# A fused attention and feed-forward kernel: a hand-woven schedule re-ordered, with sums moved from VectorE to GpSimd

## The chip, the core and the metric

The kernel runs on one core of a Trainium2 chip. The metric is the device time of one execution in microseconds (us), the median of several runs. Five engines with queues of their own work on it: TensorE (PE, matrix products), VectorE (DVE), ScalarE (ACT), GpSimd (POOL) and SyncE (SP, which issues most DMA transfers). Each engine takes its instructions strictly in the order in which the program gives them; an instruction that waits for another engine holds up everything behind it in its own queue.

## The reference

Inputs are q, k, v of shape (4 batches, 8 heads, 768 positions, 64), a decay per head, and the weights `w_in` (512 x 2048), `w_out` (2048 x 512) and `alpha` (2048).

```
for each block b of 64 positions:                        # causal linear attention with decay
    out[b]   = ((q_b k_b^T) * Dmask) v_b + (q_b * lam_pow) kv_state
    kv_state = lam^64 * kv_state + (k_b * rev_pow)^T v_b
x = out, heads side by side                              # 3072 x 512
h = x @ w_in                                             # 3072 x 2048
g = max(h, 0) + alpha * min(h, 0)
return g @ w_out                                         # 3072 x 512
```

## The kernel before

The 3072 rows are cut into six chunks `c` of 512 rows (256 positions of two batches). Every chunk goes through three steps.

**Attention.** A chunk has four groups `n` (a batch and four heads), so chunk 5 has the groups 20 to 23. `prepared(n)` casts q and k, loads v and multiplies k by its decay (`key_decayed`, GpSimd, L291). `turned(n)` transposes by DMA, `decayed(n)` multiplies the transposed q by its decay (GpSimd, L355). `cluster(old, new)` is one attention group on TensorE: the state part and the scores times v of group `old`, the scores and the new state of group `new`. Behind it VectorE masks the scores (`masked`, L402) and updates the state (`states`, L465), and ScalarE copies the result into the chunk's input for the next step (`attended`, L250).

**Up** (`up(c, f)`, L545, L553, L560): 16 pieces for a chunk, each four products 128x512 into one of two PSUM banks "h". ScalarE makes relu(-h) from the bank, then VectorE makes g from both (here "the g step"). The bank comes free with the g step, so an up piece waits for the g step of the up piece two before it.

**Down.** For the chunks 3, 4 and 5 the product g @ w_out is done with seven products of quarter matrices in place of eight (`down2`, `down2_last`, L655). A11, A12, A21, A22 are quarters of g and B11 to B22 quarters of `w_out`. Four sums of g are needed: S1 = A21 + A22, S3 = A11 - A21, S2 = S1 - A11, S4 = A12 - S2 (`g_sum`, L638; all but S1 overwrite a quarter). Each comes in four parts (0 to 3), one for every two of the eight 128-column blocks of a quarter. Four sums of weights are needed once: three new tiles W0, W1, W2 and B22 - B12 in the place of B12, called W3 here (`weight_sum`, L621), again in four parts. All of these are elementwise instructions of 128x512 values of 16 bits. The seven products are used in the order 1, 2, 6, 5, 7, 3, 4, each in two halves of eight matmuls (d = 0 to 13). Product 6 reads S2, product 5 reads S1, product 7 reads S3 and W3, product 3 reads S4, product 4 reads W2. S1 has one buffer, so the S1 of the next chunk is written after product 5 of this one.

**The order.** The queue order is written out by hand. For the last three chunks a loop weaves three things: up pieces of chunk c, down pieces of chunk c-1, and (from a table `plan`) the attention of chunk c+1. `order[c]` is a string of U (up) and D (down) pieces; for c = 4 and c = 5 it has 30 pieces with two U's side by side once in the middle. `sums_at` says after which piece a part of S2 or S4 is put in the queue, and `sums13` puts parts of S1 and S3 in the queue after the 10th, 12th, 14th and 16th up piece. The loop of c = 4 is called the woven stage below and that of c = 5 the next stage; after them `down2_last` does the down step of chunk 5 alone.

In the kernel before, S1 and S3 are on GpSimd (letter "G") and S2, S4 and all weight sums on VectorE ("V").

Of the kernel before, what the change touches and what calls it, by code (L numbers as in the profile page):

```python
# [11 lines left out]
def kernel(  # L12
# [16 lines left out]
    nc = tc.nc  # L29
# [5 lines left out]
    ALU = mybir.AluOpType  # L35
# [124 lines left out]
    for half in range(2):  # L160
# [7 lines left out]
        out=drop, in0=rel_i, scalar1=0.0, scalar2=-1e30, op0=ALU.is_lt, op1=ALU.mult  # L168
# [115 lines left out]
    def engine(x):  # L284
        return nc.gpsimd if x == "G" else nc.vector
# [82 lines left out]
    def inter(n):  # L368
        co, bo, ho = units[n]
        pbo, bb = co // 2, 2 * (co % 2) + bo  # L370
        for a in range(2):
            if 2 * pbo + a == 0:
                continue
            for hp in range(2):
                nc.tensor.matmul(  # L375
                    ot[a][:, hp, :].rearrange("p (e j) -> p e j", e=2),
                    lhsT=R[bb, ho, 2 * pbo + a][:, hp].rearrange("p l d -> p (l d)"),
                    rhs=T[n]["qdT"][:, :, hp, ds(a * 64, 64)],
                    start=(hp == 0),
                    stop=False,  # L380
                    skip_group_check=True,
                )

    def score_products(n):
        t = T[n]
        t["s"] = ps.tile([128, 2, 2, 2, L], fp32, tag="s", name="s")
        for hp in range(2):
            for e in range(2):
                for a, hl in QUADS:
                    p = ds(hl * 64, 64)  # L390
                    nc.tensor.matmul(  # L391
                        t["s"][ds(a * 64, 64), hl, hp, 1 - e, :].rearrange("p (e j) -> p e j", e=2),
                        lhsT=t["qkT"][p, 1, e, hp, ds(a * 64, 64)],
                        rhs=t["qkT"][p, 0, :, hp, ds(a * 64, 64)],
                        start=True,
                        stop=True,
                    )

    def masked(n):
        t = T[n]  # L400
        t["sm"] = sm_pool.tile([128, 2, 2, 2, L], fp16, tag="sm", name="sm")
        nc.vector.tensor_tensor(  # L402
            out=t["sm"].rearrange("p a h x j -> p (a h) x j"),
            in0=t["s"].rearrange("p a h x j -> p (a h) x j"),
            in1=mask_of(units[n][2]),
            op=ALU.mult,
        )

    def intra(n):
        t = T[n]  # L410
        pb = units[n][0] // 2
        for hp in range(2):
            for e in range(2):
                for hl, a in QUADS:
                    p = ds(a * 64, 64)
                    nc.tensor.matmul(  # L416
                        ot[a][ds(hl * 64, 64), hp, :],
                        lhsT=t["v16"][p, 2 * hp + hl, e, :],
                        rhs=t["sm"][p, hl, hp, 1 - e, :],
                        start=(2 * pb + a == 0 and hp == 0 and e == 0),  # L420
                        stop=(e == 1),
                        skip_group_check=True,
                    )
# [5 lines left out]
    def state_products(n, kv, fresh, blocks=None):  # L429
        t = T[n]  # L430
        for hp in range(2):
            for e in range(2):
                for hl in range(2):
                    for a in blocks or blocks_of(n):
                        p = ds(a * 64, 64)
                        nc.tensor.matmul(  # L436
                            kv[a][ds(hl * 64, 64), hp, hl, :],
                            lhsT=t["kdec"][p, e, 2 * hp + hl, :],
                            rhs=t["v16"][p, 2 * hp + hl, e, :],
                            start=(fresh and hp == 0 and e == 0),  # L440
                            stop=(e == 1),
                            skip_group_check=True,
                        )

    def attended(n, eng):
        co, bo, ho = units[n]
        if co not in XT:
            XT[co] = xt_pool.tile([128, NHP, 2, 2, L], fp16, tag="xT", name="xT")
        copy_on(
            eng,  # L450
            XT[co][:, ds(2 * ho, 2), :, bo, :].rearrange("p h e (a j) -> p a (h e) j", a=2),
            acc[:, :, 0:256].rearrange("p a (he j) -> p a he j", j=64),
        )
# [24 lines left out]
    def cluster(old, new, eng="A"):  # L478

        if old is not None:  # L480
            inter(old)
        if new is not None:
            score_products(new)
        if old is not None:
            intra(old)
        if new is not None:
            state_products(new, kv_acc, old is None)
            masked(new)
        if old is not None:
            attended(old, eng)  # L490
        if new is not None:
            states(new, kv_acc)
# [35 lines left out]
    G = {}  # L528
# [83 lines left out]

    halves = [[w_out_sb[:, ds(8 * x, 8), ds(256 * y, 256)] for y in range(2)] for x in range(2)]

    def weight_sum(i, part):

        p = ds(2 * part, 2)
        (b11, b12), (b21, b22) = [[y[:, p] for y in x] for x in halves]
        w = [sums[x][:, p] for x in range(3)]
        out, in0, in1 = [(w[0], b12, b11), (w[1], b22, w[0]), (w[2], b21, w[1]), (b12, b22, b12)][i]  # L620
        nc.vector.tensor_tensor(out=out, in0=in0, in1=in1, op=ALU.subtract)  # L621

    def part_of(c, j, half, e, b=None):
        x = group_of(c, j)[:, half, :, e]
        return x.rearrange("p i b j -> p i (b j)") if b is None else x[:, :, b]

    def g_sum(c, i, j, eng, b=None):

        a11, a12, a21, a22 = [part_of(c, j, half, e, b) for e in range(2) for half in range(2)]
        s1 = sums[3].rearrange("p f (b j) -> p f b j", b=2)[:, ds(2 * j, 2)]  # L630
        s1 = s1.rearrange("p i b j -> p i (b j)") if b is None else s1[:, :, b]
        out, in0, in1, op = {
            1: (s1, a21, a22, ALU.add),
            3: (a21, a11, a21, ALU.subtract),
            2: (a11, s1, a11, ALU.subtract),
            4: (a12, a12, a11, ALU.subtract),
        }[i]
        engine(eng).tensor_tensor(out=out, in0=in0, in1=in1, op=op)  # L638
# [82 lines left out]
    def sums13(c, j, eng="G"):  # L721
        g_sum(c, 1, j, eng)
        g_sum(c, 3, j, eng)
# [303 lines left out]
    def prepared(n):  # L1027
        casts(n, "AA")

    def turned(n):  # L1030
        transposes(n, "D", False)

    plan = {
        3: {
            0: lambda: (turned(18), load(5, 0, "k"), load(5, 0, "q"), decayed(17)),
            2: lambda: prepared(19),
            4: lambda: cluster(16, 17),
            7: lambda: (turned(19), decayed(18)),
            10: lambda: prepared(20),
            11: lambda: cluster(17, 18),  # L1040
            13: lambda: (turned(20), decayed(19), load(5, 1, "k"), load(5, 1, "q")),
# [6 lines left out]
        },  # L1048
        4: {
            2: lambda: prepared(23),  # L1050
            4: lambda: cluster(20, 21),
            7: lambda: (turned(23), decayed(22)),
            11: lambda: cluster(21, 22),
            13: lambda: decayed(23),
            18: lambda: cluster(22, 23),
            25: lambda: cluster(23, None),
        },
        5: {},
    }
    order = {c: "U" + "DU" * 7 + "U" + "DU" * 7 for c in plan}  # L1060
    order[3] = "UD" * 16
    sums_at = {3: (2, 0), 4: (2, 1), 5: (2, 2), 6: (2, 3), 11: (4, 0), 12: (4, 1), 13: (4, 2), 14: (4, 3)}
    sum_tiles()
    for c, at in plan.items():
        u = d = 0
        for x, what in enumerate(order[c]):
            if x in at:
                at[x]()
            if what == "U":
                up(c, u // 2 + 8 * (u % 2), None, "h")  # L1070
                u += 1
                if u in (10, 12, 14, 16):
                    sums13(c, u // 2 - 5)
            elif c == 3:
                down(c - 1, d // 4, d % 4, 4, ("op", "tk")[d // 4 % 2])
                d += 1
                if d > 2 and d <= 14:
                    weight_sum(*divmod(d - 3, 4))
            else:
                down2(c - 1, d)  # L1080
                d += 1
            if c > 3 and x in sums_at:
                g_sum(c - 1, *sums_at[x], "V")
            if c == 4 and 7 <= x <= 10:
                weight_sum(3, x - 7)
    down2_last(NC - 1)


# [28 lines left out]
```

## Time and profile before

| | |
|---|---|
| median of 3 runs | 209.15 us (208.95 to 209.23) |
| profiled execution | 209.0 us, of which 207.1 us are the span from the first to the last instruction |
| TensorE busy | 200.2 us (97% of the span) |
| VectorE busy | 158.4 us (76%) |
| ScalarE busy | 113.6 us (55%) |
| GpSimd busy | 112.6 us (54%) |
| granted TensorE clock, mean | 0.997 |

The profile is one execution. Busy time of TensorE is modelled at the ends of matmuls, so how fast TensorE goes is better read from the start times of its pieces. In a timeline a row gives start, duration, engine, line and operation, and in brackets how long the engine was idle before it and who released it.

### The profile page before, as it was taken

The page shows a single profiled execution, that of the slowest core. Times are in us where ns is not written, and L with a number is a line of the kernel's source. Part 1 is how long each engine was busy: PE and PEld are TensorE (multiplying, and loading weights), DVE is VectorE, ACT ScalarE, POOL GpSimd, SP SyncE. Part 2 cuts the span into 40 slices and gives each one's busy share as a digit, 9 for nine tenths or more (in the row PEclk, how much of TensorE's full clock was granted, in tenths as well). Part 3 has the DMA queues.
Part 4 walks back from the last instruction along what each step waited for, and adds up shares of the span by engine and source line. Part 5 has one row for each costly group of instructions (what it writes and reads, how often), then busy time and mean ns, then how long its engine had stood idle before and what let it go on. Part 6 is the DMA issues. An engine that isn't in the chain of part 4 may idle for free.

```text
span 207.1 us, 5564 instructions
## 1 busy us (share of the span) xinstructions
PE 200.2 (97%) x2263; PEld 121.4 (59%) x2263; DVE 158.4 (76%) x285; ACT 113.6 (55%) x210; POOL 112.6 (54%) x134
## 2 busy tenths in 40 slices
PE   7999999999999999999999999998999999999993
PEld 6776445556445465555555455475667666666782
DVE  7978889477789657899989996769976467855740
ACT  7986778154777118656757456472553544534221
POOL 8999793054486883294447985292074140462400
PEclk9999999999999999999999999999999999999998
DMA  5999999997999996989899973151101111011122
GB/s 154 281 195 232 246 260 207 234 285 230 244 257 265 200 259 142 235 134 172 138 138 264 229 151 89 25 114 12 54 3 51 66 38 51 2 51 59 47 101 101
DMA packets 58061, 31.16 MB, mean 150 GB/s; under 512 B 27108, under 2 KB 55796, under 8 KB 58036
## 3 DMA queue, kind: packets, MB, share of 16 engines
q1 hardware_dynamic: 42884, 21.25, 42.4%
q0 software_dynamic: 15136, 9.57, 29.0%
q8 instruction: 17, 0.28, 0.6%
q14 instruction: 8, 0.07, 0.1%
q10 hardware_dynamic: 16, 0.00, 0.0%
HBM read 27.27 MB, written 6.29 MB: 162 GB/s over the span
## 4 chain that ended last, share of the span: by engine, by line
PE 83%; DVE 10%; ACT 2%; issue 2%; POOL 1%; POOLq 1%; ACTq 0%
PE h_ps L545 37%; PE o_ps L573 19%; PE o_ps L655 14%; PE s L391 3%; PE acc L416 3%; PE acc L375 2%; DVE g L638 2%; DVE g L560 2%; DVE sm L402 2%; PE tpx L341 2%; DVE dmask L202 1%; PE acc L436 1%; DVE R L465 1%; DVE w_out_sb L621 1%; ACT L180 1%
## 5 line engine op out<-in xcount | busy, mean ns | idle before, releaser
L545 PE MATMUL h_ps<-xT,w_in_sb 128*128 128x512 f16 (+1 forms) x392 | 92.1, 375 | 1.0 <-DVE g L560 0.8
L560 DVE SCALAR_TENSOR_TENSOR g<-m,oma,h_ps 128x512 f16<-128x512 f32 (+1 forms) x98 | 71.1, 733 | 26.5 <-ACT m L553 23.5
L553 ACT ACTIVATE m<-h_ps 128x512 f32<-128x512 f32 (+1 forms) x98 | 57.3, 588 | 49.0 <-PE h_ps L545 44.7
L545 PEld LDWEIGHTS <-w_in_sb 128*128 128x128 f16 x392 | 37.5, 98 | 38.5 <-issue 1.7
L573 PE MATMUL o_ps<-w_out_sb,g 128*128 128x512 f16 x192 | 46.8, 380 | 0.0
L402 DVE TENSOR_TENSOR sm<-s,dmask 128x1024 f16<-128x1024 f32 x24 | 29.2, 1218 | 11.4 <-PE s L391 11.4
L638 POOL TENSOR_TENSOR s<-g 128x512 f16<-128x512 f16 x12 | 14.4, 1198 | 40.5 <-DVE g L560 25.7
L655 PEld LDWEIGHTS <-g 128*128 128x128 f16 x288 | 27.7, 98 | 9.2 <-DVE g L638 0.8
L573 PEld LDWEIGHTS <-g 128*128 128x128 f16 x192 | 17.6, 98 | 19.4 <-DVE g L560 0.2
L250 ACT ACTIVATE xT<-acc 128x512 f16<-128x512 f32 x24 | 14.3, 598 | 23.4 <-PE acc L436 20.4
L355 POOL TENSOR_TENSOR qdT<-qkT,qdecay 128x512 f16<-128x512 f16 (+1 forms) x19 | 20.9, 1107 | 6.0 <-DMA qkT<-qk 6.0
L655 PE MATMUL o_ps<-w_out_sb,g 128*128 128x256 f16 x192 | 24.1, 273 | 0.0
L291 POOL TENSOR_TENSOR kdec<-kraw,kdecay 128x512 f16<-128x512 f32 x18 | 19.5, 1088 | 6.6 <-DMA kraw<-in_k_dram 6.5
L254 POOL CAST qk<-qraw 128x512 f16<-128x512 f32 x12 | 7.8, 652 | 17.6 <-DMA qraw<-in_q_dram 17.6
L465 DVE SCALAR_TENSOR_TENSOR R<-R,rdecay,acc 128x128 f16<-128x128 f16 x54 | 15.4, 339 | 0.1
L278 POOL DMA_DIRECT2D v<-in_v_dram x19 | 14.9, 791 | 0.4 <-issue 0.4
L638 POOL TENSOR_TENSOR g<-g 128x512 f16<-128x512 f16 x12 | 14.1, 1171 | 0.9
L685 ACT ACTIVATE o_sb<-o_ps 128x512 f32<-128x512 f32 (+1 forms) x16 | 7.9, 491 | 11.7 <-PE o_ps L655 11.7
L655 PE MATMUL o_ps<-w_sum,g 128*128 128x256 f16 x96 | 12.6, 273 | 0.3 <-DVE g L638 0.3
L391 PE MATMUL s<-qkT 64*64 64x128 f16 x384 | 10.1, 221 | 0.1
L416 PE MATMUL acc<-sm,v 64*64 64x128 f16 x384 | 9.8, 218 | 0.1
L254 POOL CAST qk<-kraw 128x512 f16<-128x512 f32 x9 | 5.5, 613 | 6.7 <-DMA kraw<-in_k_dram 3.9
(80 smaller groups left out, 191.6 us busy)
## 6 DMA issues: line engine op xcount, KB each, us to landing
out_dram<-o_sb SPq DMA_DIRECT2D x20, 256.0 KB, 2.8
kraw<-in_k_dram SPq DMA_DIRECT2D x7, 512.0 KB, 5.5
qraw<-in_q_dram SPq DMA_DIRECT2D x6, 512.0 KB, 5.7
v<-in_v_dram POOLq DMA_DIRECT2D x19, 128.0 KB, 6.0
w_in_sb<-in_moe_w_in_dram POOLq DMA_DIRECT2D x4, 512.0 KB, 8.5
w_out_sb<-in_moe_w_out_dram POOLq DMA_DIRECT2D x4, 512.0 KB, 10.6
qraw<-in_q_dram POOLq DMA_DIRECT2D x6, 256.0 KB, 7.2
qraw<-in_q_dram SPq DMA_DIRECT2D x6, 256.0 KB, 4.6
```

Source lines behind the costliest of these rows:

```text
L291: engine(eng).tensor_tensor(out=kdec, in0=kr, in1=kdecay[:, ds(4 * hh, 4), :].rearrange("p h e -> p e h").unsqueeze(3).to_broadcast([128, ...
L355: engine(eng).tensor_tensor(out=qdT[:, :, :, p], in0=(t["qps"] if eng == "P" else t["qkT"][:, 0])[:, :, :, p], in1=qdecay[:, hh, :, :, p], ...
L391: nc.tensor.matmul(t["s"][ds(a * 64, 64), hl, hp, 1 - e, :].rearrange("p (e j) -> p e j", e=2), lhsT=t["qkT"][p, 1, e, hp, ds(a * 64, 64)] ...
L402: nc.vector.tensor_tensor(out=t["sm"].rearrange("p a h x j -> p (a h) x j"), in0=t["s"].rearrange("p a h x j -> p (a h) x j"), in1=mask_of ...
L416: nc.tensor.matmul(ot[a][ds(hl * 64, 64), hp, :], lhsT=t["v16"][p, 2 * hp + hl, e, :], rhs=t["sm"][p, hl, hp, 1 - e, :], start=(2 * pb + a ...
L465: nc.vector.scalar_tensor_tensor(out=R[b, hh, m + 1][:, hp], in0=R[b, hh, m][:, hp], scalar=rdecay[:, 2 * hh + hp : 2 * hh + hp + 1], in1= ...
L545: nc.tensor.matmul(h_ps[:, 0:n] if bi is None else h_ps[:, 0:n].rearrange("p (e j) -> p e j", e=2), lhsT=w_in_sb[:, gi, ts(f, 128)], rhs=x ...
L553: nc.scalar.activation(m[:, 0:n], h_ps[:, 0:n], AF.Relu, scale=-1.0)
L560: nc.vector.scalar_tensor_tensor(out=g, in0=mv, scalar=oma[:, f : f + 1], in1=hv, op0=ALU.mult, op1=ALU.add)
L573: nc.tensor.matmul(o_ps, lhsT=lhs(c, f, t), rhs=w_out_sb[:, f, :], start=(f == 0), stop=(f == NF - 1),)
L638: engine(eng).tensor_tensor(out=out, in0=in0, in1=in1, op=op)
L655: nc.tensor.matmul(t[:, cols], lhsT=x, rhs=w, start=(fresh and f == 0), stop=(last and f == NF // 2 - 1), skip_group_check=True,)
```

## The change

For the woven stage (c = 4) and the next stage (c = 5):

- the two U's side by side move from the pieces 14 and 15 to 18 and 19 of the 30 (counted from 0);
- the attention groups in c = 4 go from in front of the pieces 4, 11, 18 and 25 to in front of 8, 14, 22 and 28;
- in c = 4, the parts 1 and 3 of S2 and all of S4 go to GpSimd, and S4 from the pieces 11 to 14 to the pieces 15, 17, 19 and 21;
- in c = 5, S2 stays and S4 goes to the pieces 11, 13, 15 and 17, still on VectorE;
- W2 goes from VectorE in the loop of c = 3 to GpSimd in c = 4 (after the pieces 10, 12, 14 and 16), W3 from the pieces 7 to 10 to 10 to 13, still on VectorE;
- the last part of S1 and S3 (chunk 5, after its last up piece) goes from GpSimd to VectorE.

```diff
-    def weight_sum(i, part):
+    def weight_sum(i, part, eng="V"):
...
-        nc.vector.tensor_tensor(out=out, in0=in0, in1=in1, op=ALU.subtract)
+        engine(eng).tensor_tensor(out=out, in0=in0, in1=in1, op=ALU.subtract)
...
         4: {
             2: lambda: prepared(23),
-            4: lambda: cluster(20, 21),
             7: lambda: (turned(23), decayed(22)),
-            11: lambda: cluster(21, 22),
+            8: lambda: cluster(20, 21),
             13: lambda: decayed(23),
-            18: lambda: cluster(22, 23),
-            25: lambda: cluster(23, None),
+            14: lambda: cluster(21, 22),
+            22: lambda: cluster(22, 23),
+            28: lambda: cluster(23, None),
         },
         5: {},
     }
-    order = {c: "U" + "DU" * 7 + "U" + "DU" * 7 for c in plan}
+    order = {c: "U" + "DU" * 9 + "U" + "DU" * 5 for c in plan}
     order[3] = "UD" * 16
-    sums_at = {3: (2, 0), 4: (2, 1), 5: (2, 2), 6: (2, 3), 11: (4, 0), 12: (4, 1), 13: (4, 2), 14: (4, 3)}
+    sums_at = {
+        4: {3: (2, 0, "V"), 4: (2, 1, "G"), 5: (2, 2, "V"), 6: (2, 3, "G")},
+        5: {3: (2, 0, "V"), 4: (2, 1, "V"), 5: (2, 2, "V"), 6: (2, 3, "V")},
+    }
+    for x in range(4):
+        sums_at[4][15 + 2 * x] = (4, x, "G")
+        sums_at[5][11 + 2 * x] = (4, x, "V")
...
                 if u in (10, 12, 14, 16):
-                    sums13(c, u // 2 - 5)
+                    sums13(c, u // 2 - 5, "V" if c == 5 and u == 16 else "G")
...
-                if d > 2 and d <= 14:
+                if d > 2 and d <= 10:
                     weight_sum(*divmod(d - 3, 4))
...
-            if c > 3 and x in sums_at:
-                g_sum(c - 1, *sums_at[x], "V")
-            if c == 4 and 7 <= x <= 10:
-                weight_sum(3, x - 7)
+            if x in sums_at.get(c, {}):
+                g_sum(c - 1, *sums_at[c][x])
+            if c == 4 and 10 <= x <= 13:
+                weight_sum(3, x - 10)
+            if c == 4 and x in (10, 12, 14, 16):
+                weight_sum(2, x // 2 - 5, "G")
```

## The prediction

> **What bounds the kernel now.** I read the page first, for the engine that is never idle, and then three views of the woven stage: TensorE's timeline, the busy time by stretches, and the chain of waits.
>
> ```profile
> PE 200.2 (97%) x2263; PEld 121.4 (59%) x2263; DVE 158.4 (76%) x285; ACT 113.6 (55%) x210; POOL 112.6 (54%) x134
> ```
>
> TensorE has something in hand for 97% of the span, so only what holds TensorE up can move the time. Its timeline, by the starts of pieces:
>
> ```profile
> 133.53 1.03 PE L545 MATMUL h_ps<-xT,w_in_sb 128*128 128x512 f16 x4
> ...
> 137.00 0.39 PE L375 MATMUL acc<-qdT,R 128*128 128x128 f16 x4
> ...
> 138.01 1.04 PE L545 MATMUL h_ps<-xT,w_in_sb 128*128 128x512 f16 x4
> ...
> 140.62 1.04 PE L655 MATMUL o_ps<-w_out_sb,g 128*128 128x256 f16 x8
> 142.29 1.02 PE L545 MATMUL h_ps<-xT,w_in_sb 128*128 128x512 f16 x4 [0.64 <-DVE g L560]
> ...
> 159.56 0.39 PE L375 MATMUL acc<-qdT,R 128*128 128x128 f16 x4
> ...
> 160.22 1.04 PE L545 MATMUL h_ps<-xT,w_in_sb 128*128 128x512 f16 x4
> ...
> 163.71 1.89 PE L545 MATMUL h_ps<-xT,w_in_sb 128*128 128x512 f16 x8
> ...
> 190.61 3.66 PE L655 MATMUL o_ps<-w_out_sb,g 128*128 128x256 f16 x32
> ```
>
> The woven stage begins at 133.53. From 163.71, its last up piece, to 190.61 lie 31 pieces (that one and the 30 of the next stage): 26.90 / 31 = 0.868 us each, the price of a piece when nothing waits. A group with a new one costs 1.01 (137.00 to 138.01), the last group 0.66 (159.56 to 160.22). So the 29 pieces from 133.53 should take 29 x 0.868 = 25.17, and the groups 3 x 1.01 + 0.66 = 3.69, in all 28.86. They took 163.71 - 133.53 = 30.18. **The woven stage loses 1.32 us**, 0.80 of it between 140.62 and 142.29, where an up piece waits for a g step on VectorE; the next stage loses nothing.
>
> Why VectorE is late, from the chain of waits and the table by stretches (length, then PE, PEld, DVE, ACT, POOL):
>
> ```profile
> 137.62 2.13 DVE g L638
> ```
> ```profile
> 142.30:150.90 8.60, 8.46 (x90) 5.26 (x90) 8.60 (x19) 3.58 (x6) 0.00 (x0) 1.00 0.10 32
> ```
>
> One part of S2 sits on VectorE for over 2 us, and after it VectorE has no free moment for 8.60 us, while GpSimd does nothing at all. That is the backlog at which the change aims. VectorE's own rows give the prices:
>
> ```profile
> 131.41 0.41 DVE L621 TENSOR_TENSOR w_sum<-w_out_sb,w_sum 128x512 f16<-128x512 f16 x1
> 131.77 0.75 DVE L560 SCALAR_TENSOR_TENSOR g<-m,oma,h_ps 128x512 f16<-128x512 f32 x1
> ...
> 135.22 0.75 DVE L560 SCALAR_TENSOR_TENSOR g<-m,oma,h_ps 128x512 f16<-128x512 f32 x1 [0.98 <-ACT m L553]
> 136.96 0.75 DVE L560 SCALAR_TENSOR_TENSOR g<-m,oma,h_ps 128x512 f16<-128x512 f32 x1 [0.99 <-ACT m L553]
> 137.62 2.31 DVE L638 TENSOR_TENSOR g<-s,g 128x512 f16<-128x512 f16 x1
> ...
> 141.51 0.73 DVE L560 SCALAR_TENSOR_TENSOR g<-m,oma,h_ps 128x512 f16<-128x512 f32 x1
> ...
> 147.09 1.21 DVE L402 TENSOR_TENSOR sm<-s,dmask 128x1024 f16<-128x1024 f32 x1
> ...
> 148.74 0.41 DVE L638 TENSOR_TENSOR g<-g 128x512 f16<-128x512 f16 x1
> ```
>
> Rows overlap a little, so I take the step from one start to the next. A sum costs 0.36 (131.41 to 131.77), a g step 0.66 (136.96 to 137.62), mask and state of a group together 1.65 (147.09 to 148.74). A g step starts 1.69 after its up piece (133.53, 135.22); the up piece that needs its bank starts 0.12 after the g step's end (141.51 + 0.66 = 142.17, then 142.29).
>
> **The same sum costs 0.36 or 2.3, and GpSimd decides which.** Two places in the stage before, VectorE first, then GpSimd:
>
> ```profile
> 115.14 1.82 DVE L621 TENSOR_TENSOR w_sum<-w_out_sb 128x512 f16<-128x512 f16 x1
> ...
> 118.85 0.72 DVE L621 TENSOR_TENSOR w_sum<-w_out_sb,w_sum 128x512 f16<-128x512 f16 x1
> 119.49 0.73 DVE L560 SCALAR_TENSOR_TENSOR g<-m,oma,h_ps 128x512 f16<-128x512 f32 x1
> ```
> ```profile
> 114.50 1.06 POOL L291 TENSOR_TENSOR kdec<-kraw,kdecay 128x512 f16<-128x512 f32 x1
> 115.52 1.16 POOL L638 TENSOR_TENSOR s<-g 128x512 f16<-128x512 f16 x1
> ...
> 117.94 1.34 POOL L355 TENSOR_TENSOR qdT<-qkT,qdecay 128x512 f16<-128x512 f16 x1
> 119.25 1.34 POOL L638 TENSOR_TENSOR s<-g 128x512 f16<-128x512 f16 x1
> ```
>
> The sum at 118.85 arrives while GpSimd works, and ends at 119.49, which is 0.24 after GpSimd's next instruction began (119.25); GpSimd's step becomes 1.31 (117.94 to 119.25). So a VectorE sum that meets a busy GpSimd waits for the end of GpSimd's instruction, slips in, and delays GpSimd by 0.20 against the 1.11 below. The sum at 115.14 shows the worse case: it met kdec at 114.50 and ended only at 116.96, behind the next instruction as well. The 2.31 at 137.62 is the same, behind kdec too.
>
> **Part 1: the end of the kernel, a gain.** TensorE, then VectorE, at the last chunk:
>
> ```profile
> 194.10 0.82 PE L655 MATMUL o_ps<-w_sum,g 128*128 128x256 f16 x6
> 195.21 1.26 PE L655 MATMUL o_ps<-w_sum,g 128*128 128x256 f16 x10 [0.29 <-DVE g L638]
> 196.35 1.91 PE L655 MATMUL o_ps<-w_sum,s 128*128 128x256 f16 x16
> 198.09 2.78 PE L655 MATMUL o_ps<-w_out_sb,g 128*128 128x256 f16 x24
> ```
> ```profile
> 192.10 1.65 DVE L638 TENSOR_TENSOR g<-s,g 128x256 f16<-128x256 f16 x3
> 194.87 1.10 DVE L638 TENSOR_TENSOR g<-s,g 128x256 f16<-128x256 f16 x5 [1.11 <-POOL g L638]
> ```
>
> Sixteen matmuls took 196.35 - 194.10 = 2.25, the next sixteen 198.09 - 196.35 = 1.74: 0.51 lost, because the last part of S2 waits for S1 and S3 on GpSimd. With S1 and S3 on VectorE after the last g step (192.10) they cost 2 x 0.36, and four half parts of S2 at most 4 x 0.36: done by 194.3, while TensorE wants the last part at 194.10 + 6 / 16 x 1.74 = 194.75. GpSimd is then idle, so nothing blocks these. **Gain 0.51.** What can go in all is 1.32 + 0.51 = 1.83.
>
> **Part 2: GpSimd's new queue.** Its rows in the woven stage:
>
> ```profile
> 134.32 1.15 POOL L638 TENSOR_TENSOR s<-g 128x512 f16<-128x512 f16 x1 [4.12 <-DVE g L560]
> 135.55 1.15 POOL L638 TENSOR_TENSOR g<-g 128x512 f16<-128x512 f16 x1
> 136.65 0.80 POOL L278 DMA_DIRECT2D v<-in_v_dram  x1
> 137.47 1.06 POOL L291 TENSOR_TENSOR kdec<-kraw,kdecay 128x512 f16<-128x512 f32 x1
> 138.49 1.16 POOL L355 TENSOR_TENSOR qdT<-qkT,qdecay 128x512 f16<-128x512 f16 x1
> ...
> 152.56 1.15 POOL L638 TENSOR_TENSOR g<-g 128x512 f16<-128x512 f16 x1
> 153.67 1.15 POOL L638 TENSOR_TENSOR s<-g 128x512 f16<-128x512 f16 x1
> ```
>
> A GpSimd step is 1.11 (152.56 to 153.67), 1.23 for S1, whose S3 follows it (134.32 to 135.55). From 138.49 the new queue is: S2(1), S2(3), q decay, W2(0), W2(1), q decay, W2(2), S4(0), W2(3), S4(1), S1, S3, S4(2), S1, S3, S4(3). I find nothing there that still waits for its inputs, so it runs without a gap: 14 x 1.11 + 2 x 1.23 = 18.00, to 156.49. Six VectorE sums fall into it (S2(0), S2(2), W3 four times); each delays it by 0.20: 157.7. The first half of product 3 is piece 22, behind three groups: 133.53 + 22 x 0.868 + 3.03 = 155.66, and wants S4(3) at three quarters, 156.31. So **GpSimd alone costs TensorE 1.4**, or 0.2 if none of the six came between.
>
> The Trainium skill speaks against such moves: "GPSIMD Engine Reference", Engine selection, puts elementwise work on VectorE and calls GpSimd about twice as slow with two inputs. Here 1.11 stands against 0.36, three times. By the page's factor, as an estimate, a step would be 0.72, this floor would vanish, and the time would come near that of the third rival below; I go by the rows.
>
> **Part 3: VectorE's new queue.** Piece 10, the sixth up piece, starts at 133.53 + 10 x 0.868 + 1.01 = 143.22; its g step at 144.91, ending at 145.57. Behind it stand W3(0), W3(1), a g step, W3(2), W3(3), mask and state, and the g step of the eighth up piece, for whose bank the tenth, piece 18, waits. GpSimd, by its queue with two delays, starts W2(2) at 138.49 + 6 x 1.11 + 0.40 = 145.55, just ahead of W3(0). So W3(0) ends 0.24 behind the next GpSimd start, at 146.90. Then GpSimd starts every 1.31: 147.97, 149.28, 150.59. W3(1) ends at 148.21, the g step at 148.87, W3(2) at 149.52, W3(3) at 150.83, mask and state at 152.48, the g step at 153.14, and piece 18 starts at 153.26. Unhindered it would start at 133.53 + 18 x 0.868 + 2.02 = 151.17. **Cost 2.09.** It hides the 1.4 of GpSimd, since product 3 comes later by as much. The relief of six sums fewer on VectorE in this stage is thus eaten by the waits of those left there.
>
> The early S2(0) still waits for some 2.2 at 137.62 (kdec, then S2(1)), but the group's mask is no longer behind it, and the up piece in danger has 0.9 to spare. W2's removal from the stage of chunk 2 frees VectorE where TensorE lost nothing. The cover for the last `attended` is two pieces, 1.74 in front of the next stage. In that stage S4 now runs before GpSimd's S1 and S3 begin. I cost these three at nothing; without their cover each is worth up to half a microsecond.
>
> **The sum.** 2.09 - 1.83 = +0.26: the profiled execution would have a span of 207.4 in place of 207.1 (1.9 lies around it), the median 209.15 + 0.26 = 209.4. A run of this kernel can be told from no change from 0.2%, 0.42 us, on: this is no measurable change.
>
> **Rivals.** First, a lost race: W2(2) is due at 145.55 and W3(0) at 145.57, too close to call. If VectorE goes first, W3(0) ends at 145.9 and the chain shortens by one GpSimd step: piece 18 loses 0.97, GpSimd's floor of 1.4 then decides, and the sum is 1.4 - 1.83 = -0.4, 208.7.
>
> Second, slower: VectorE loses to GpSimd's following instruction too, as at 115.14. For are two rows, both behind kdec; against is 118.85, behind a q decay. From two of the four W3 waits doubled on, piece 18 is later by 2 x 1.11 or more: 211.6; with one, 210.5.
>
> Third, faster: the queues interleave without harm, because the waits of W3 fall into gaps that I don't see. Then only GpSimd's 0.2 is left: 0.2 - 1.83 = -1.6, 207.5. Against it: six sums and no gap in the queue. The Trainium skill, "SBUF — State Buffer", two separate sides, has whichever of the two engines starts first hold the shared port for its whole instruction, which the 2.31 here bears out.
>
> **Numbers.** The forecast 0.45 (with some 0.4 us of error either way), the lost race 0.20, the double waits 0.20, no harm 0.15. Faster by over 0.2% comes from no harm and over half of the lost race: 0.27. Slower from the double waits and a third of the forecast: 0.34. The rest, 0.39, is within. The range 208.2 to 210.6 holds the forecast, the lost race and one double wait; it leaves out most of no harm and the far end of the double waits. The forecast's own range is 209.0 to 209.8.
>
> **What would show it.** In the changed profile: GpSimd without a gap from 134.3 to about 157; W3 rows of 0.6 to 1.4 in place of 0.41; one stall of an up piece near 151 to 153, released by a g step; no stall at 142 nor at 195. Wrong would be: W3 rows of 0.41, a busy but harmless GpSimd, or a stall in product 3 that outweighs the up piece's.

## The result and the profile after

The changed kernel takes 215.14 us (median of 5 runs, 215.03 to 215.47) against 209.15 us: the ratio is 1.0287, 95% interval 1.0267 to 1.0307. It is 6.0 us slower, where the prediction had 209.4 us and a range of 208.2 to 210.6. The profiled execution took 215.47 us with a span of 213.5 us.

The page of the changed kernel, busy times and then the line of the granted TensorE clock in 40 slices:

```profile
PE 201.9 (95%) x2263; PEld 122.8 (58%) x2263; DVE 163.1 (76%) x277; ACT 113.5 (53%) x210; POOL 120.8 (57%) x142
...
PEclk9999999999999999999999999995799999999999
```

Before, that line was full but for the last slice (0.8); now two slices in the middle show half and 0.7. TensorE's timeline says where:

```profile
133.72 1.03 PE L545 MATMUL h_ps<-xT,w_in_sb 128*128 128x512 f16 x4
...
140.67 0.39 PE L375 MATMUL acc<-qdT,R 128*128 128x128 f16 x4
...
147.48 1.87 PE L545 MATMUL h_ps<-xT,w_in_sb 128*128 128x512 f16 x4 [5.73 <-DVE g L560]
149.14 1.91 PE L655 MATMUL o_ps<-w_sum,g 128*128 128x256 f16 x8
150.85 1.54 PE L545 MATMUL h_ps<-xT,w_in_sb 128*128 128x512 f16 x4
152.22 1.04 PE L655 MATMUL o_ps<-w_sum,g 128*128 128x256 f16 x8
...
170.57 1.89 PE L545 MATMUL h_ps<-xT,w_in_sb 128*128 128x512 f16 x8
...
200.97 1.91 PE L655 MATMUL o_ps<-w_sum,g 128*128 128x256 f16 x16
202.72 1.91 PE L655 MATMUL o_ps<-w_sum,s 128*128 128x256 f16 x16
```

The woven stage now runs from 133.72 to its last up piece at 170.57: 36.85 us, where 28.86 us would do. Of the 7.99 us lost, one stall takes 5.80: the attention group ends at 141.68, and the fifth up piece starts at 147.48. The three pieces behind it take 1.66, 1.71 and 1.37 in place of 0.868 each, 2.14 more. The table by stretches (the column before the last two is the granted clock) shows why:

```profile
141.70:147.48 5.78, 0.05 (x4) 0.07 (x1) 5.78 (x3) 0.60 (x1) 5.42 (x6) 0.79 0.00 0
147.48:149.14 1.66, 1.66 (x4) 0.54 (x4) 1.66 (x3) 0.00 (x0) 1.66 (x2) 0.50 0.00 0
149.14:150.85 1.71, 1.71 (x10) 1.18 (x8) 1.71 (x4) 0.60 (x1) 1.26 (x2) 0.50 0.24 81
150.85:152.22 1.37, 1.37 (x5) 0.54 (x4) 0.99 (x3) 0.00 (x0) 0.00 (x0) 0.63 0.29 102
152.22:153.09 0.87, 0.87 (x9) 0.78 (x8) 0.04 (x1) 0.60 (x1) 0.00 (x0) 1.00 0.00 0
```

So a part of the loss comes behind the stall: TensorE was granted half its clock. By finer stretches the clock fell at 145.05, 3.4 us after the attention group's end, and came back at 151.87, 4.4 us after TensorE had resumed. The Trainium skill, "TensorE: Matmul & The Clock Gate", Part 1: The HAM clock gate, says the clock is halved after an idle window of about 3.4 us and comes back after a busy window of about that length; the fall agrees here, and the return took 1.0 us more.

Elsewhere the stalls of before are gone: there is no other in the stage, and the sixteen matmuls near the end take 202.72 - 200.97 = 1.75 in place of 2.25. So the sum is 7.99 - 1.32 - 0.51 = +6.2, against +6.0 between the medians and +6.4 between the two profiled spans.

The stall comes from one instruction. VectorE's timeline, then GpSimd's:

```profile
137.15 0.75 DVE L560 SCALAR_TENSOR_TENSOR g<-m,oma,h_ps 128x512 f16<-128x512 f32 x1 [0.99 <-ACT m L553]
137.82 8.96 DVE L638 TENSOR_TENSOR g<-s,g 128x512 f16<-128x512 f16 x1
146.69 0.73 DVE L560 SCALAR_TENSOR_TENSOR g<-m,oma,h_ps 128x512 f16<-128x512 f32 x1
```
```profile
136.84 0.80 POOL L278 DMA_DIRECT2D v<-in_v_dram  x1
137.66 1.06 POOL L291 TENSOR_TENSOR kdec<-kraw,kdecay 128x512 f16<-128x512 f32 x1
138.67 2.26 POOL L638 TENSOR_TENSOR g<-s,g 128x512 f16<-128x512 f16 x2
140.90 1.15 POOL L355 TENSOR_TENSOR qdT<-qkT,qdecay 128x512 f16<-128x512 f16 x1
142.02 2.25 POOL L621 TENSOR_TENSOR w_sum<-w_out_sb,w_sum 128x512 f16<-128x512 f16 x2
144.23 1.15 POOL L355 TENSOR_TENSOR qdT<-qkT,qdecay 128x512 f16<-128x512 f16 x1
145.35 1.14 POOL L621 TENSOR_TENSOR w_sum<-w_out_sb,w_sum 128x512 f16<-128x512 f16 x1
146.85 1.15 POOL L638 TENSOR_TENSOR g<-g 128x512 f16<-128x512 f16 x1 [0.36 <-DVE g L638]
```

S2(0), a sum of 0.36 us, lasts 8.96 us. GpSimd runs kdec and seven more instructions past it, without a gap. S2(0) is let in only when GpSimd comes to S4(0), which itself needs S2(0) and so waits. The g step of the third up piece is queued behind S2(0) on VectorE, and the fifth up piece waits for that step's bank.

### The profile page after: what moved, and what is told of

It is laid out like the page before. It is cut to its first block, busy times and chain, and to the rows that moved or that the text cites. A ratio compares the mean times of both kernels' runs of the same rounds, so it can differ in the third digit from the quotient of the medians.

```text
span 213.5 us, 5566 instructions
## 1 busy us (share of the span) xinstructions
PE 201.9 (95%) x2263; PEld 122.8 (58%) x2263; DVE 163.1 (76%) x277; ACT 113.5 (53%) x210; POOL 120.8 (57%) x142
## 4 chain that ended last, share of the span: by engine, by line
PE 78%; DVE 11%; issue 5%; ACT 3%; ACTq 0%; DVEq 0%
PE h_ps L545 34%; PE o_ps L573 17%; PE o_ps L655 16%; DVE g L560 4%; PE s L391 3%; PE acc L416 2%; DVE sm L402 2%; PE acc L375 2%; PE tpx L341 1%; ACT m L553 1%; DVE w_sum L621 1%; DVE dmask L202 1%; DVE R L465 1%; PE acc L436 1%; ACT L180 1%
## 5 line engine op out<-in xcount | busy, mean ns | idle before, releaser
L545 PE MATMUL h_ps<-xT,w_in_sb 128*128 128x512 f16 (+1 forms) x392 | 93.3, 379 | 6.1 <-DVE g L560 6.1
L655 PEld LDWEIGHTS <-g 128*128 128x128 f16 x288 | 28.4, 99 | 9.0 <-issue 0.7
L638 POOL TENSOR_TENSOR s<-g 128x512 f16<-128x512 f16 x11 | 12.8, 1167 | 32.4 <-DVE g L560 16.2
L573 PEld LDWEIGHTS <-g 128*128 128x128 f16 x192 | 17.6, 98 | 19.4 <-DVE g L560 0.2
L638 POOL TENSOR_TENSOR g<-g 128x512 f16<-128x512 f16 x15 | 17.5, 1172 | 1.2 <-DVE g L638 0.4
L638 DVE TENSOR_TENSOR g<-s,g 128x256 f16<-128x256 f16 (+1 forms) x14 | 13.2, 989 | 0.0
L655 PE MATMUL o_ps<-w_sum,g 128*128 128x256 f16 x96 | 13.2, 285 | 0.0
```

What stands on the lines that cost most here:

```text
L545: nc.tensor.matmul(h_ps[:, 0:n] if bi is None else h_ps[:, 0:n].rearrange("p (e j) -> p e j", e=2), lhsT=w_in_sb[:, gi, ts(f, 128)], rhs=x ...
L573: nc.tensor.matmul(o_ps, lhsT=lhs(c, f, t), rhs=w_out_sb[:, f, :], start=(f == 0), stop=(f == NF - 1),)
L655: nc.tensor.matmul(t[:, cols], lhsT=x, rhs=w, start=(fresh and f == 0), stop=(last and f == NF // 2 - 1), skip_group_check=True,)
```

## The experiments

| kernel | median, us | ratio to before (95%) | length of S2(0), us |
|---|---|---|---|
| changed kernel | 215.14 | 1.0287 (1.0267 to 1.0307) | 8.96 |
| kdec_early | 213.87 | 1.0218 (1.0151 to 1.0286) | 7.96 |
| s2_all_g | 215.80 | 1.0310 (1.0274 to 1.0346) | (on GpSimd) |
| before_w2_g | 216.66 | 1.0352 (1.0327 to 1.0377) | 7.85 |
| w2_back | 210.88 | 1.0088 (1.0071 to 1.0105) | 5.65 |
| load_early | 208.58 | 0.9963 (0.9942 to 0.9983) | 0.42 |
| gap_behind_load | 209.22 | 1.0009 (0.9994 to 1.0025) | 1.21 |
| load_early_w2_back | 207.22 | 0.9899 (0.9883 to 0.9916) | 0.42 |
| before_load_early | 207.82 | 0.9921 (0.9902 to 0.9940) | 0.42 |
| before_tail | 208.53 | 0.9968 (0.9956 to 0.9981) | 2.32 |
| before_load_tail | 207.42 | 0.9922 (0.9910 to 0.9935) | 0.42 |

### What shuts VectorE out: kdec, the row, or the load?

In the trace of before, both long waits stood behind kdec, and the prediction blamed kdec. Two other theories fit. Theory row: any row of GpSimd instructions without a gap does it. Theory load: the v load in front of kdec does it (rows at 113.68 and 136.65 of before). Four runs were to tell them apart.

The first is no version of the kernel but twelve rows of GpSimd instructions with one VectorE sum against each. In outline:

```
for kind, gap, load, later in CASES:       # gap: VectorE steps before its sum
    go = VectorE step;  GpSimd: sum that reads go
    if load: GpSimd issues a v load
    GpSimd: one instruction of `kind`, then five of `later`, all independent
    VectorE: `gap` steps, then one sum of two 16-bit inputs
```

> This kernel computes nothing of the reference; it puts one VectorE sum (two 16-bit inputs, 128x512) against a row of six GpSimd instructions that wait for nothing, twelve times over, and writes zeros. The cases differ in the first GpSimd instruction of the row (a sum of 16-bit values, the key decay kdec with its fp32 inputs, a cast, or a product with one fp32 input), in what follows it, in when the VectorE sum arrives, and in whether a v load stands in front. Theory kdec (a request that falls into kdec loses to all that GpSimd has in its queue): the VectorE sum takes 0.4 to 1.4 us where it meets a sum or a cast, and 5 us or more where it meets kdec. Theory row (any GpSimd row without a semaphore wait shuts VectorE out until it ends): 5 us or more in every case. Theory load (the v load in front is what does it): 5 us only in the three cases with a load.

VectorE's timeline for four cases: a row of sums, a row that begins with kdec, then load and kdec, and load and sums:

```profile
7.73 1.26 DVE L38 TENSOR_TENSOR sum<-a,a 128x512 f16<-128x512 f16 x1
...
25.41 1.15 DVE L38 TENSOR_TENSOR sum<-a,a 128x512 f16<-128x512 f16 x1
...
44.48 6.05 DVE L38 TENSOR_TENSOR sum<-a,a 128x512 f16<-128x512 f16 x1
...
54.11 6.04 DVE L38 TENSOR_TENSOR sum<-a,a 128x512 f16<-128x512 f16 x1
```

kdec is innocent: behind it VectorE waits for one instruction, as behind any other (all nine cases without a load: 0.42 to 1.27 us). With a load in front, with kdec or without, the sum waits for the end of the row (6.04 to 6.72 in the three cases).

> The changed kernel with one instruction moved: the key decay of group 23 goes from the woven stage to the end of the stage before, where GpSimd idles for some 4 us. The first S2 part on VectorE then meets S2(1) or the v load on GpSimd in place of kdec. Theory kdec: that part takes at most 1.3 us in place of 8.96, the stall of 5.7 us before the fifth up piece and the lowered clock behind it go, and the time falls to 207.5 to 209.5 us. Theory row: GpSimd's row is as dense as before, the part still takes 6 us or more, and the time stays above 213 us.

```diff
-        key_decayed(n)
+        if n != 23:
+            key_decayed(n)
...
-            28: lambda: (turned(22), decayed(21)),
+            28: lambda: (turned(22), decayed(21), key_decayed(23)),
```

With kdec out of the row, theory kdec fails here too: S2(0) takes 7.96 us, less by one GpSimd instruction, and the time is 213.87 us. Theory row would pass this run, but not the cases above.

> The changed kernel with S2(0) and S2(2) of the woven stage on GpSimd as well, so no VectorE sum is left in the dense stretch until W3(0) near 145.6 us. Both theories: the stall before the fifth up piece and the low clock go. Theory kdec: each W3 part waits for one GpSimd instruction (0.6 to 1.4 us), S4(3) comes 2.2 us later and holds product 3 by 2 to 3 us: 209 to 211 us. Theory row: W3(0) is shut out until GpSimd waits for product 5 or ends its row, 4 us or more, and a new stall of 3 us or more stands at the tenth up piece: 211 to 213 us.

```diff
-        4: {3: (2, 0, "V"), 4: (2, 1, "G"), 5: (2, 2, "V"), 6: (2, 3, "G")},
+        4: {3: (2, 0, "G"), 4: (2, 1, "G"), 5: (2, 2, "G"), 6: (2, 3, "G")},
```

With no S2 on VectorE the next sum in its queue takes the blow. VectorE's timeline, then GpSimd's:

```profile
145.92 8.94 DVE L621 TENSOR_TENSOR w_out_sb<-w_out_sb 128x512 f16<-128x512 f16 x2
```
```profile
152.16 1.14 POOL L638 TENSOR_TENSOR s<-g 128x512 f16<-128x512 f16 x1
153.37 2.51 POOL L638 TENSOR_TENSOR g<-g 128x512 f16<-128x512 f16 x2
```

W3(0) and W3(1) together last 8.94 us, although seven more GpSimd instructions lay between the load (136.96) and its arrival. W3(0) gets in after 153.30, where S3 (153.37) has to wait for S1. The expected 211 to 213 us for theory row was short: 215.80.

> The kernel before with one part of the change alone: W2 on GpSimd in the woven stage. GpSimd then has q decay, two W2, q decay and two W2 in one row behind kdec, while S2(0) on VectorE is in its old place and meets kdec. Both theories: S2(0) takes 7 to 8 us in place of 2.31, the up piece behind it stalls by 5 us or more, the granted clock falls behind the stall, and the time rises to 213 to 216 us. If instead only the six sums moved together do the harm: within 0.5 us of 209.15.

```diff
-                if d > 2 and d <= 14:
+                if d > 2 and d <= 10:
...
+            if c == 4 and x in (10, 12, 14, 16):
+                weight_sum(2, x // 2 - 5, "G")
```

W2 alone, put on GpSimd in the kernel before, costs 7.3 us against the 209.38 of the kernel before in the same runs, more than expected: S2(0) takes 7.85 us, to the end of GpSimd's row (145.45).

### Taking the load away

> The changed kernel with one instruction moved: the v load of group 23, which GpSimd issues, goes from the woven stage to the end of the stage before, where GpSimd idles; kdec stays. Theory load (a load issued by GpSimd shuts VectorE's two-input sums out until GpSimd's row has a true gap): S2(0) takes at most 1.4 us in place of 8.96, the stall before the fifth up piece and the low clock go, and the W3 parts wait for one GpSimd instruction each, as the prediction had it: 208.0 to 209.8 us. Theory kdec or theory row: S2(0) still takes 7 us or more: above 213 us.

```diff
-            28: lambda: (turned(22), decayed(21)),
+            28: lambda: (turned(22), decayed(21), load_v16(23)),
```

VectorE's timeline, with S2(0), and then the two pairs of W3; then GpSimd's row beside them; then the one stall that is left, from TensorE's:

```profile
137.69 0.42 DVE L638 TENSOR_TENSOR g<-s,g 128x512 f16<-128x512 f16 x1
...
145.66 1.92 DVE L621 TENSOR_TENSOR w_out_sb<-w_out_sb 128x512 f16<-128x512 f16 x2
147.50 0.73 DVE L560 SCALAR_TENSOR_TENSOR g<-m,oma,h_ps 128x512 f16<-128x512 f32 x1
148.16 2.02 DVE L621 TENSOR_TENSOR w_out_sb<-w_out_sb 128x512 f16<-128x512 f16 x2
```
```profile
136.74 1.05 POOL L291 TENSOR_TENSOR kdec<-kraw,kdecay 128x512 f16<-128x512 f32 x1
...
144.84 1.16 POOL L621 TENSOR_TENSOR w_sum<-w_out_sb,w_sum 128x512 f16<-128x512 f16 x1
145.96 1.34 POOL L638 TENSOR_TENSOR g<-g 128x512 f16<-128x512 f16 x1
147.26 1.34 POOL L621 TENSOR_TENSOR w_sum<-w_out_sb,w_sum 128x512 f16<-128x512 f16 x1
148.55 1.34 POOL L638 TENSOR_TENSOR g<-g 128x512 f16<-128x512 f16 x1
```
```profile
150.39 1.04 PE L655 MATMUL o_ps<-w_out_sb,g 128*128 128x256 f16 x8
152.53 1.89 PE L545 MATMUL h_ps<-xT,w_in_sb 128*128 128x512 f16 x8 [1.10 <-DVE g L560]
```

One DMA issue moved six pieces ahead turns 215.14 into 208.58 us. What remains is the prediction's own mechanism: GpSimd's row goes on without a gap, but each W3 part waits for one instruction of it, and the tenth up piece stalls, by 152.53 - 150.39 - 0.868 = 1.27. The short S2(0) alone proves less: without the 0.80 us of the load's issue kdec starts earlier, and S2(0) arrives 0.1 us before its end. The W3 parts, which arrive while GpSimd works, and the run with a gap below do not have this flaw.

> The kernel before with that v load moved and nothing else. Theory load: S2(0) waits for the rest of kdec alone, 1.0 to 1.4 us in place of 2.31, so that VectorE's backlog starts 1 us smaller and of the 1.32 us lost in the woven stage 0.5 to 1.0 goes: 208.1 to 208.7 us. Theory kdec or row: S2(0) stays at 2.3 us and the time within 0.2 us of the kernel before.

The kernel before with that line alone: S2(0), at 139.24, arrives just as kdec ends (138.29 + 1.05 = 139.34) and slips in behind it, and the time falls to 207.82 us, more than expected. The woven stage takes 164.18 - 135.15 = 29.03 us in this trace and so loses 0.17 in place of 1.32: what the kernel before lost here was nearly all due to where the load stood, by the shut-out and by its 0.80 us in GpSimd's row together.

> As load_early, and W2 goes back to VectorE in the stage of chunk 2, so that GpSimd's row is shorter by four instructions and W3 meets less of it. Theory load: S2(0) at most 1.4 us, W3 parts 0.4 to 1.3 us, no stall of an up piece above 0.5 us, and the 0.51 of the end gained: 207.0 to 208.3 us, faster than both kernels. Theory kdec or row: S2(0) 4 to 6 us, a stall of 2 us or more, 211 us or more.

```diff
-                if d > 2 and d <= 10:
+                if d > 2 and d <= 14:
...
-            if c == 4 and x in (10, 12, 14, 16):
-                weight_sum(2, x // 2 - 5, "G")
```

With W2 back as well, the W3 pairs take 0.76 us each and no piece stalls: 207.22 us, 1.0% faster than the kernel before and the lowest median measured.

### When the shut-out begins and ends

> This kernel computes nothing of the reference; eight rows of nine GpSimd sums against one VectorE instruction, with zeros written. Theory load: without a load 0.4 to 1.5 us; with a load near the head of the row, VectorE's sum lasts to the row's end, also when it arrives two or three instructions after the load; with a load in the middle it lasts to the end if it arrives with the load, and 0.4 to 1.5 us if it arrives before; with the same load issued by SP, 0.4 to 1.5 us; a VectorE addition with one input in PSUM takes 0.6 us whatever GpSimd does. If each GpSimd sum reads the sum before it, the gaps between them let VectorE in within 1.5 us in spite of the load. If the load works only on a sum that waits at that moment, the late arrival takes 0.4 to 1.5 us.

The eight cases are rows of nine GpSimd sums. VectorE's timeline, in their order:

```profile
7.74 1.26 DVE L38 TENSOR_TENSOR sum<-a,a 128x512 f16<-128x512 f16 x1
...
20.35 8.35 DVE L38 TENSOR_TENSOR sum<-a,a 128x512 f16<-128x512 f16 x1
...
33.86 6.67 DVE L38 TENSOR_TENSOR sum<-a,a 128x512 f16<-128x512 f16 x1
...
44.89 7.45 DVE L38 TENSOR_TENSOR sum<-a,a 128x512 f16<-128x512 f16 x1
...
55.92 0.50 DVE L38 TENSOR_TENSOR sum<-a,a 128x512 f16<-128x512 f16 x1
...
67.71 0.48 DVE L38 TENSOR_TENSOR sum<-a,a 128x512 f16<-128x512 f16 x1
...
78.76 0.48 DVE L38 TENSOR_TENSOR sum<-a,a 128x512 f16<-128x512 f16 x1
...
91.39 0.68 DVE L89 TENSOR_TENSOR sum<-a,bank 128x512 f16<-128x512 f16 x1
```

In turn: no load; a load near the head; the same with VectorE two instructions later (6.67, still to the row's end); a load in the middle; a load and then sums that each read the one before (0.50: their gaps let VectorE in); a load issued by SP (0.48); a GpSimd load that comes after the sum (0.48); and, with a GpSimd load, an addition with one input in PSUM (0.68). So the shut-out lasts for as long as GpSimd goes on without a gap, it holds for late arrivals too, and a VectorE instruction with one SBUF input is not touched. It is not the transfer itself that keeps VectorE out: in the second case the sum ends 10 us after the load's issue (18.60 to 28.70), where the loads of this run land a median of 3.2 us after theirs.

The SP case is no test. That load waits for nothing, so SP issued it at 1.23 us, over 60 us before its row, and the case is one more row without a load. Nearer evidence is in load_early: SP issued a DMA transpose at 136.36 and a store at 141.87 within GpSimd's gapless row, and the sums behind them waited for one GpSimd instruction at most. A v load issued by SP beside such a row was not run.

> The changed kernel with everything in its place and one small GpSimd instruction more (128x64, unread), right behind kdec, that reads kdec's result and so has to wait for it, as S3 waits for S1. Theory load, with a gap as what ends the shut-out: S2(0) is let in at this gap, takes 1.0 to 1.7 us in place of 8.96, and the time falls to that of the kernel with the load moved, 208.2 to 209.4 us, although GpSimd's row is longer than in the changed kernel. If so short a wait doesn't end it: S2(0) at 8 us or more and 214 us or more.

```diff
         key_decayed(n)
+        if n == 23:
+            x = const.tile([128, 64], fp16, name="gap")
+            nc.gpsimd.tensor_tensor(out=x, in0=T[n]["kdec"][:, 1, 3], in1=ident[:, 0:64], op=ALU.mult)
```

GpSimd's timeline, then VectorE's:

```profile
137.20 0.80 POOL L278 DMA_DIRECT2D v<-in_v_dram  x1
138.02 1.06 POOL L291 TENSOR_TENSOR kdec<-kraw,kdecay 128x512 f16<-128x512 f32 x1
139.16 0.38 POOL L307 TENSOR_TENSOR gap<-kdec,ident 128x64 f16<-128x64 f16 x1
```
```profile
138.17 1.21 DVE L641 TENSOR_TENSOR g<-s,g 128x512 f16<-128x512 f16 x1
```

A gap of 0.08 us (139.08 to 139.16) in the changed kernel, made by one unread instruction, is enough: S2(0) gets in behind kdec, and the time is 209.22 us. The load and the whole row keep their order, which makes this the cleanest of the runs.

### The change in its parts

> The changed kernel with W2 back on VectorE in the stage of chunk 2 and the v load in its place. Theory load: GpSimd's row behind the load is kdec, two S2 parts and two q decays, and then S4(0) waits for S2(0), so S2(0) is let in near 143 us and takes 5 to 5.6 us in place of 8.96; the fifth up piece stalls by 2 to 3 us. With the 1.83 us that the change takes away, that is 209.3 to 210.6 us without a loss of clock, and up to 2 us more if so short a stall lowers the clock too. If W2 on GpSimd was the whole cause: S2(0) at 0.4 to 1.4 us, 207 to 208 us.

This is load_early_w2_back without the load moved. S2(0) takes 5.65 us, until S4(0) on GpSimd has to wait for it near 143.0, and the fifth up piece stalls for 2.44 us. The clock falls in this shorter stall as well, 2.0 us after the attention group's end (141.45 to 143.41), sooner than the 3.4 us of the Trainium skill would have it, and comes back at 146.83. The table by stretches:

```profile
144.50:146.00 1.50, 1.50 (x6) 0.61 (x4) 1.50 (x4) 0.14 (x1) 1.26 (x1) 0.50 0.04 11
```

Two pieces take 1.66 and 1.47, 1.39 more than 2 x 0.868, so that 2.44 + 1.39 - 1.83 = +2.0 stands against +1.8 measured.

> The kernel before with one part of the change alone: the last part of S1 and S3 on VectorE. It should be worth the 0.51 us that the prediction read from the sixteen matmuls at the end: 0.4 to 0.6 us less than the kernel before, and the sixteen matmuls in 1.75 us in place of 2.25. If the end is bound by something else (ScalarE's copies, the output's transfers), under 0.1 us.

> The kernel before with the v load moved and the last S1 and S3 on VectorE, and with no other part of the change: no re-ordering, no S2, S4 or W2 on GpSimd. If the re-ordering and the sums on GpSimd bring what is left of load_early_w2_back's gain, it stays above that kernel by 0.5 us or more (207.7 and up). If the shut-out by the load was nearly all of the loss in the woven stage, it comes within 0.4 us of it: 207.0 to 207.6.

```diff
-                    sums13(c, u // 2 - 5)
+                    sums13(c, u // 2 - 5, "V" if c == 5 and u == 16 else "G")
```

The last S1 and S3 on VectorE alone give 208.53 us, 0.59 below the 209.12 of the kernel before in the same runs; the sixteen matmuls take 1.75. With the load moved too, and nothing re-ordered, the time is 207.42 us. This is within the range expected if the load was nearly all of the loss. The intervals of this kernel and of load_early_w2_back meet (0.9910 to 0.9935 and 0.9883 to 0.9916), and the medians differ by 0.2 us, so no gain of the re-ordering and of the S2 and S4 sums on GpSimd is shown.

## Why the prediction was wrong

**What bounds the kernel, and what could be gained: right.** The 1.32 us of the woven stage and the 0.51 at the end were there to be had. Part 1 is shown by itself (0.59 us measured).

**The step that failed is the price of S2(0) in Part 3**, costed at "some 2.2" and then at nothing: it measured 8.96 us. Behind it stands the reading of the rows at 115.14 and 118.85. I read a wait for the end of GpSimd's current instruction as the rule, and the longer wait as a habit of kdec. The rows allowed that: kdec stood in both. But so did the load, one row further up in GpSimd's timeline, and I had left out that row at 113.68, since a DMA issue counts as no work. The runs show another rule: behind a load, VectorE waits for a gap, however long the row, and the change made the row long. It also fits the two waits of before: at 116.75 S3 had to wait for S1, 0.07 us behind its end, and behind 139.65 GpSimd had to wait for a DMA until 140.67. Part 2 found that the new queue has no gap and priced only what TensorE waits for at its end.

**The second rival had the right kind of mechanism and the wrong size.** It let VectorE lose to one instruction more, in the W3 sums. It was S2(0) that lost, to seven more. The sentence that this is the same "behind kdec too" should have raised the question of what ends such a wait.

**The granted clock was missing** from every case: 2.14 of the 7.99 us lost in the stage. A stall of TensorE of some microseconds must be priced with the slow pieces behind it.

**The rest of Part 3, without the shut-out, was right in kind and too high.** In load_early the W3 parts each wait for one instruction and the tenth up piece stalls, as written, but by 1.27 in place of 2.09: the four parts took 3.8 us (145.66 to 147.50, 148.16 to 150.10), where the prediction had 4.6. W3(0) came near the end of a GpSimd instruction (146.00), not near the start of one, which is the race of the first rival. GpSimd's floor of 1.4 did not bind there, in a row without the load's 0.80 us. In gap_behind_load, with the load in its place, the stall is 1.19, and product 3 loses 0.5 us more to S4(3), so the stall did not hide all of that floor. Without the shut-out the changed kernel thus takes 208.6 us with the load moved and 209.2 with it in place. That the second is close to the forecast of 209.4 does not vindicate its terms.

**The shared port** was read as a lock for one instruction. The Trainium skill, "SBUF — State Buffer", Who interferes with whom, has an instruction hold the port for its own length, by which S2(0) would have waited for the instruction in progress. The rows without a load agree (0.42 to 1.27); those with one do not (5.65 to 8.96), and the measurement decides. The 2.31 of before, which the prediction took to bear this out, already spoke against it: S2(0) waited for the rest of kdec and for the whole q decay behind it.

Open: why a load does this. The runs show when the shut-out begins and ends, not what in GpSimd holds the port.

## What to carry to other kernels

Moving work from VectorE to GpSimd is not free for VectorE: while GpSimd works, a VectorE sum with two SBUF inputs waits for GpSimd's instruction, and behind a v load that GpSimd issued it waits for the whole gapless row. Put such a load where a gap follows it (in front of an instruction that has to wait), or make a gap; issuing it from another queue was not tested. When one instruction's duration varies by more than its work, look at the other engine's rows before it, DMA issues included, until one rule explains every case.

## What the runs showed of the hardware

Behind a v load issued by GpSimd (it casts to 16 bits; no other kind of DMA was tried), GpSimd's instructions keep VectorE's two-input 16-bit sums out until GpSimd first has a gap. The sum of 0.36 us took 5.65 to 8.96 us in the rows of five or more instructions, against 0.42 to 1.27 us in the test rows without a load. A wait of GpSimd of 0.08 us ended it.

A stall of TensorE of 2.44 us was enough to halve the granted clock, and one of 1.10 us was not (1.00 behind the stall in load_early). The clock fell 2.0 us into the stall in w2_back, 3.4 in the changed kernel and 5.2 in before_w2_g, and stayed at half for 3.4, 6.8 and 6.8 us.
